# Value products in 64x32 tiles, exponentials in three tiles of 512, and the pair ring in free-first order

## The chip, the core and the metric

The kernel runs on one core of one Trainium2 chip. The metric is device time in microseconds, the median of several executions. Shorter is better.

## The reference

One layer mixes a sliding-window attention A and a dense MLP B, both on the same x (2048 rows of 512), by a gate that is one number per row:

```python
x = A_x
g = sigmoid((x * gate_w).sum(-1, keepdims=True))
# A: 32 heads of 16, causal, each query sees itself and the 255 keys before it
qkv = (x @ wqkv).reshape(B, S, 3, H, Dh)            # S = 2048, D = 512
scores = einsum("bhqd,bhkd->bhqk", q, k) * (Dh ** -0.5)
mask = (i - j >= 0) & (i - j < 256)
p = softmax(where(mask, scores, -1e9))
a = (einsum("bhqk,bhkd->bhqd", p, v)).reshape(B, S, D) @ wo
# B: F = 1792
b = gelu(x @ w1 + b1) @ w2 + b2
return g * a + (1 - g) * b
```

## The kernel before, in words

**Two kinds of work on TensorE.** The dense products (query/key and value projections `qk` and `v`, MLP `u` and `y`, output projection `a`) split each fp32 operand into a rounded high part and a remainder, and add three products. They run as pairs of matmuls with 64 contraction rows each, 512 columns wide: rows 0 to 63 work on one output bank and rows 64 to 127 on another, side by side (`half`, L689 to L702; `Dense`, which chooses what each half does next). The attention runs in 32 units, one for each of 4 query blocks of 512 (c) and 8 groups of 4 heads (g_).

**One attention unit.** (1) `att_max` (`sm`, L865) computes scores of 128 queries by 384 keys, and VectorE finds each query's maximum (L871, L872). (2) `att_rows` writes the negated maxima as extra rows of the queries, so that the next product comes out with them subtracted. (3) `att_exp` (`st`, L928) computes the scores again with keys on partitions and queries on the free axis, ScalarE takes the exponential into a tile `pt` (L933), and GpSimd zeroes the triangles of it that the window excludes (L937, two calls a tile). A unit sees up to six key blocks kb = 0 to 5 of 128 keys; block 2 is the first one of the query block itself. `PARTS` lays them out in four tiles of 384 queries a head pair: kb 0 and 1 (128 and 256 queries), kb 2 (384), kb 3 (384), kb 4 and 5 (256 and 128). (4) `att_pv` (`pv`, L957) multiplies values by exponentials: four heads in four 128x32 column tiles of the array, 128 key rows each, all six key blocks accumulated in one bank of ring `d`. These operands are plain fp32, and the trace has two matmul records for each such matmul, called passes below. (5) ScalarE copies the bank out (L970), a DMA sends it to `ND`, and numerators and denominators go through DRAM to the division. In the 8 units of c = 0, kb 0 and 1 do not exist: tile 0 is left out there.

**PSUM.** Ring `d` has 4 banks, used by the dense groups and by `pv`. Ring `sc` has 2 pairs of banks, used by `sm` and `st`, and by the transposes of x.

**Order of the work.** All five queues are filled by a planner in the kernel itself (`Plan`, with `op`, `pe`, `ready`, `advance`): every operation carries a cost in ns, and the planner writes each engine's program in the order that its own clock makes ready. The main loop gives TensorE, at each step, either the next attention item (`score_items` lists them in one fixed order) when its inputs and its bank are ready by the plan and attention is due, or a pair of dense halves, or one half alone. At run time each queue is in order, so an instruction whose semaphore is late holds what stands behind it on its engine. `Ring` gives buffers out in turn; `Slots` gives the buffer that comes free first.

**The end.** After the last `pv`, dense halves of the output projection `a` of the third query block fill TensorE while the last heads go through `att_last` (DRAM, reciprocal, product, split). Then come 48 matmuls of 128 rows (`whole`, L803) for the last query block, of which the last 12 need the last heads.

Of the kernel before, what the change touches and what calls it, by code (L numbers as in the profile page):

```python
# [18 lines left out]
T = 512  # L19
NT = S // T  # L20
NB = T // 128
# [5 lines left out]
SCALE = DH ** -0.5  # L27
# [144 lines left out]
def gated_mix(ctx: ExitStack, tc: tile.TileContext, x, wqkv, wo, w1, b1, w2, b2, gate_w, out):  # L172
    nc = tc.nc
    x = x[0]
    out = out[0]
# [8 lines left out]
    plan = Plan()  # L184
    op, pe = plan.op, plan.pe
# [133 lines left out]
    def load_two(k, prio):  # L319
        tag = "pt" if k < 2 * NB else "raw"  # L320

        def start(n):
            for i in (n, n + 1) if n == k else ():
                if tag == "pt":
                    v = new("pt", [128, 2, 384], F32, f"xr{i}", toks["xr", i], toks["z", i])
# [387 lines left out]
    class Dense:  # L713
# [1 line left out]


        def __init__(self, groups):
            self.groups, self.at, self.opened = groups, 0, 0
# [14 lines left out]
        def ready(self, g_, r):  # L733

            group = self.groups[g_]
            t = plan.ready(needs(group.mms[self.k[r][g_]][0]), [rings["d"]] if group.p is None else [])
            if t is None:
                return None
            return max(t, self.touch[1 - r][g_] + APART)
# [171 lines left out]
    PARTS = [[(0, 0, 128), (1, 0, 256)], [(2, 0, 384)], [(3, 128, 384)], [(4, 256, 256), (5, 384, 128)]]  # L911

    def parts_at(j):
        return [(*p, sum(v[2] for v in PARTS[j][:n])) for n, p in enumerate(PARTS[j])]

    def att_exp(i, j, pr):
        q, k = qbuf[:, i % QB], kbuf[:, i % QB]
        rel, box = Tok(), []

        def go():  # L920
            pt = new("pt", [128, 2, 384], F32, f"pt{i}_{j}_{pr}", toks["pv", i])
            pts[i, j, pr] = pt
            p = pair(f"st{i}_{j}_{pr}", rel)
            box.extend((pt, p))
            for kb, lo, w, at in sorted(parts_at(j), key=lambda v: -v[2]):
                for s in range(2):
                    rows_ = slice(64 * s, 64 * s + KR)
                    nc.tensor.matmul(p[:, s, at:at + w], k[rows_, pr, kb * 128:(kb + 1) * 128],  # L928
                                     q[rows_, pr, lo:lo + w], start=True, stop=True, skip_group_check=True)
        done = pe(SPAIR + (0 if j in (1, 2) else 46), go)  # L930
        if j == 3 and pr == 1:
            toks["stacks", i].t = done.t
        op({"ACT": 810.0}, lambda e: nc.scalar.activation(box[0], box[1][:, :, :384], AF.Exp, scale=SCALE), [done], 0, rel)  # L933

        def keep(at, upper):
            v = box[0][:, :, at:at + 128]
            nc.gpsimd.affine_select(out=v, in_=v, pattern=[[0, 2], [1 if upper else -1, 128]], compare_op=ALU.is_ge,  # L937
                                    fill=0.0, base=0 if upper else -1, channel_multiplier=-1 if upper else 1)
        k0 = op({"POOL": 440.0}, lambda e: keep(0, j > 0), [rel], 2)
        op({"POOL": 440.0}, lambda e: keep(256, j == 3), [k0], 2, toks["pt", i, j, pr])  # L940

    def att_pv(i):
        c, g_ = combos[i]
        vt = vbuf[:, i % 2]
        rel, box = Tok(), []
        tiles = range(1 if c == 0 else 0, 4)
        cost = 2950 if c else 2300

        def go():
            pv = bank(f"pv{i}", rel, tag=PVT)  # L950
            box.append(pv)
            first = True
            for j in tiles:
                at = 0
                for n, (kb, lo, w) in enumerate(PARTS[j]):
                    for h in range(4):
                        nc.tensor.matmul(pv[32 * h:32 * h + 32, lo:lo + w],  # L957
                                         vt[:, 68 * kb + 17 * h:68 * kb + 17 * h + 32],
                                         pts[i, j, h // 2][:, h % 2, at:at + w],
                                         start=first, stop=j == 3 and n == 1,  # L960
                                         skip_group_check=True, tile_position=(0, 32 * h))
                    first = False
                    at += w
        done = pe(cost, go)
        toks["pv", i].t = done.t
        box2 = []

        def ev(e):
            box2.append(new("tmp", [128, T], F32, f"nd{i}", sent))
            nc.scalar.activation(box2[0], box[0], AF.Copy)  # L970
        sent = ND_T[i] = Tok()
        te = op({"ACT": 595.0}, ev, [done], EVP[4], rel, [rings["tmp"]])
# [70 lines left out]
    def score_items():  # L1043

        NU = len(combos) * NB
        for u in range(-LEAD, NU):
            i, j = divmod(u, NB)
            mi, mj = divmod(u + LEAD, NB)
            if mj == LOADAT and mi + AHEADQ < len(combos):
                yield 0, [], [], lambda mi=mi: att_load(mi + AHEADQ), 0  # L1050
            if j == 0 and i >= 0:
                yield 0, [], [], lambda i=i: att_load_v(i), 0
            for pr in range(2):
                if mi < len(combos):
# [3 lines left out]
                if i >= 0 and (j > 0 or combos[i][0] > 0):  # L1058
                    yield 180, [toks["rows", i]], [rings["sc"], rings["pt"]], lambda i=i, j=j, pr=pr: att_exp(i, j, pr), 1
                if i > 0 and j == PVAT and pr == 0:  # L1060
                    yield 2700, pv_needs(i - 1), [rings[PVT]], lambda i=i: att_pv(i - 1), 2
        yield 2700, pv_needs(NU // NB - 1), [rings[PVT]], lambda: att_pv(NU // NB - 1), 2

    def pv_needs(i):
        js = range(1 if combos[i][0] == 0 else 0, 4)
        return [toks["lv", i]] + [toks["pt", i, j, pr] for j in js for pr in range(2)]


    def main():
# [17 lines left out]
        box = []  # L1087
# [16 lines left out]
            att_load(i)  # L1104
        dense = Dense(groups)
        score = score_items()
        A_all = 128 * 2 * (176 + 184) + 32 * 2700.0
        a_at = 0.0
        a = next(score, None)
        LEADA = dense.total * (1 - ENDS)  # L1110
# [2 lines left out]
        while a or not dense.over():  # L1113
# [14 lines left out]
            ra = plan.ready(a[1], a[2]) if a else None  # L1128
            can = dense.pick(t)
            a_ok = ra is not None and ra <= t  # L1130
            due = a and (dense.over() or a_at / A_all <= dense.spent / LEADA)
# [89 lines left out]
```

## Time and profile before

| what | value |
|---|---|
| median of 3 runs | 714.04 us (713.48 to 714.2) |
| the profiled execution | 715.14 us |
| its span, first to last instruction | 713.4 us |
| TensorE busy | 99% of the span |
| VectorE, ScalarE, GpSimd busy | 73%, 66%, 60% |
| granted TensorE clock | 1.00 |

How to read the rows of the prediction: PE is TensorE's matmuls, PEld its weight loads, DVE VectorE, ACT ScalarE, POOL GpSimd. A group's row has the line, engine, operation, output<-inputs, shapes, the count, then busy time in us, mean ns of one, and idle time ahead of them with what ended it. A timeline row begins with the start and the length in us; a chain row likewise. A row of waits has: who waited <- for whom: us in total, times, longest.

### The profile page before, as it was taken

To read this page: it belongs to the slowest core of one execution; us is meant where nothing else is said; L and a number is where in the kernel's file an instruction comes from. 1 tells how busy PE (TensorE), PEld (TensorE's weight loads), DVE (VectorE), ACT (ScalarE), POOL (GpSimd) and SP (SyncE) were. 2 spreads that over 40 slices of the span, in tenths; PEclk is the share of its full clock that TensorE was granted. 3 is DMA by queue.
4 is the path that set the end of the run, shared out by engine and by line. 5 is a ranking of instruction groups with operands and counts; after the bars stand their busy time and mean duration, and the time that the engine had idled before them with its cause. 6 is when DMAs were issued, how large, how long until landed. Compare 5 with 4: busy or idle time off the path is not lost.

```text
span 713.4 us, 18412 instructions
## 1 busy us (share of the span) xinstructions
PE 703.7 (99%) x6819; PEld 589.4 (83%) x6819; DVE 521.5 (73%) x994; ACT 473.1 (66%) x776; POOL 425.4 (60%) x777
## 2 busy tenths in 40 slices
PE   9999999999999999999999999999999999999997
PEld 7899888778887788978877888878888888878776
DVE  6377778968777886796754677895876877778655
ACT  5746688748867865865654678875875886775800
POOL 5234559755856974774633567892774896684700
PEclk9999999999999999999999999999999999999999
DMA  8896888187666666666959988765778677755554
GB/s 294 209 272 202 218 270 249 49 220 223 135 131 119 133 143 152 146 173 150 247 199 224 250 241 213 183 200 134 194 183 163 149 178 171 177 197 188 182 193 151
DMA packets 104616, 133.89 MB, mean 188 GB/s; under 512 B 38472, under 2 KB 53840, under 8 KB 104528
## 3 DMA queue, kind: packets, MB, share of 16 engines
q1 hardware_dynamic: 104528, 132.73, 70.4%
q8 instruction: 54, 0.88, 0.6%
q14 instruction: 34, 0.28, 0.1%
HBM read 82.39 MB, written 50.30 MB: 186 GB/s over the span
## 4 chain that ended last, share of the span: by engine, by line
PE 88%; DVE 3%; POOL 3%; DMA 2%; ACT 1%; issue 1%; SPq 1%; POOLq 0%; DVEq 0%; ACTq 0%
PE y L699 21%; PE u L699 19%; PE pv L957 11%; PE qk L699 10%; PE sm L865 7%; PE st L928 5%; PE v L699 5%; PE a L699 5%; PE a L803 2%; POOL qbuf L907 1%; DMA kbuf<-SK 1%; PE v L803 1%; PE qk L803 1%; PE xp L359 1%; DMA rb<-RD 1%
## 5 line engine op out<-in xcount | busy, mean ns | idle before, releaser
L937 POOL TENSOR_SCALAR_AFFINE_SELECT pt<-pt 128x256 f32<-128x256 f32 x480 | 215.0, 473 | 170.6 <-ACT pt L933 166.5
L933 ACT ACTIVATE pt<-st 128x768 f32<-128x768 f32 x240 | 194.0, 810 | 92.6 <-PE st L928 87.0
L699 PE MATMUL y<-w,h 64*128 64x512 f32 x1344 | 220.2, 397 | 0.0
L699 PEld LDWEIGHTS y<-w,h 64*128 64x128 f32 x1344 | 157.2, 185 | 13.4 <-PE y L699 1.5
L871 DVE COPY_PREDICATED sm<-lower,sm 128x256 f32<-128x256 uint8 x224 | 95.0, 424 | 92.0 <-PE sm L865 84.8
L699 PE MATMUL u<-xt,w 64*128 64x512 f32 x1008 | 161.3, 395 | 0.1
L872 DVE TENSOR_REDUCE M<-sm 128x2 f32<-128x512 f32 x224 | 154.9, 691 | 7.7
L699 PEld LDWEIGHTS u<-xt,w 64*128 64x128 f32 x1008 | 118.7, 185 | 6.8 <-PE u L699 0.7
L699 PE MATMUL qk<-xt,qk 64*128 64x512 f32 x720 | 109.9, 395 | 0.0
L865 PE MATMUL sm<-kbuf,qbuf 56*128 56x384 f32 (+2 forms) x512 | 106.3, 353 | 2.3 <-DVE xt L363 0.8
L928 PE MATMUL st<-qbuf,kbuf 56*128 56x256 f32 (+2 forms) x704 | 96.3, 284 | 0.2
L907 POOL CAST qbuf<-tt 8x256 fp32r<-8x256 f32 x171 | 78.9, 462 | 22.8 <-PE st L928 5.9
L501 POOL TENSOR_TENSOR h<-x1h,h 128x512 fp32r<-128x512 f32 x56 | 77.1, 1379 | 20.5 <-ACT h L491 20.0
L699 PEld LDWEIGHTS qk<-xt,qk 64*128 64x128 f32 x720 | 84.3, 185 | 5.4 <-ACT xr L369 0.4
L957 PE MATMUL pv<-pt,vbuf 128*32 128x384 f32 (+2 forms) x1408 | 84.3, 386 | 1.0 <-ACT x1h L474 1.0
L865 PEld LDWEIGHTS sm<-kbuf,qbuf 56*128 56x128 f32 x512 | 62.4, 184 | 23.8 <-issue 10.9
L928 PEld LDWEIGHTS st<-qbuf,kbuf 56*128 56x128 f32 x704 | 77.9, 186 | 4.3 <-POOL qbuf L907 0.8
L957 PEld LDWEIGHTS pv<-pt,vbuf 128*32 128x32 f32 x1408 | 41.5, 110 | 44.9 <-issue 29.5
L699 PE MATMUL u<-mx,w 64*128 64x512 f32 x336 | 59.3, 397 | 0.0
L487 DVE SCALAR_TENSOR_TENSOR x1h<-sqh,x1h 128x512 f32<-128x512 f32 x56 | 49.0, 880 | 7.7 <-ACT sqh L497 7.3
L484 DVE SCALAR_TENSOR_TENSOR sqh<-sqh,x1h 128x512 f32<-128x512 f32 x56 | 49.2, 882 | 2.8 <-ACT sqh L479 2.8
L474 ACT ACTIVATE x1h<-u,b1c 128x512 f32<-128x512 f32 x56 | 38.4, 686 | 17.4 <-PE u L699 12.4
(85 smaller groups left out, 816.9 us busy)
## 6 DMA issues: line engine op xcount, KB each, us to landing
kbuf<-SK SPq DMA_DIRECT2D x48, 192.0 KB
SQ<-qke SPq DMA_DIRECT2D x16, 512.0 KB
SK<-qke SPq DMA_DIRECT2D x16, 512.0 KB
qbuf<-SQ SPq DMA_DIRECT2D x64, 128.0 KB
ND<-nd SPq DMA_DIRECT2D x32, 256.0 KB
raww<-in_B_w_dram SPq DMA_DIRECT2D x28, 256.0 KB
kbuf<-SK SPq DMA_DIRECT2D x48, 96.0 KB
SV<-vx SPq DMA_DIRECT2D x16, 272.0 KB
```

The costliest lines, as they stand in the source:

```text
L484: nc.vector.scalar_tensor_tensor(box["q"], box["q"], GC, box["x"], op0=ALU.add, op1=ALU.mult)
L487: nc.vector.scalar_tensor_tensor(box["x"], box["q"], 1.0, box["x"], op0=ALU.add, op1=ALU.mult)
L501: lambda e: ENG[e].tensor_sub(hts[name][:, 1], box["x"], f32(hts[name][:, 0])), [t5], gp, toks["h", name])
L699: ins = nc.tensor.matmul(wide(group.p, rhs), lhsT[rows_], rhs[rows_], start=group.left == n, stop=group.left == 1, skip_group_check=True)
L865: nc.tensor.matmul(p[:, s, :w], q[rows_, pr, j * 128:(j + 1) * 128], k[rows_, pr, at:at + w], start=True, stop=True)
L871: nc.vector.copy_predicated(p[:, :, 0:128], lower.unsqueeze(1).broadcast_to([128, 2, 128]), p[:, :, 256:384])
L872: nc.vector.tensor_reduce(M[:, j, 2 * pr:2 * pr + 2], p[:, :, 0:256], AXES, ALU.max)
L907: nc.gpsimd.tensor_copy(dst, src)
L928: nc.tensor.matmul(p[:, s, at:at + w], k[rows_, pr, kb * 128:(kb + 1) * 128], q[rows_, pr, lo:lo + w], start=True, stop=True, skip_group_c ...
L933: op({"ACT": 810.0}, lambda e: nc.scalar.activation(box[0], box[1][:, :, :384], AF.Exp, scale=SCALE), [done], 0, rel)
L937: nc.gpsimd.affine_select(out=v, in_=v, pattern=[[0, 2], [1 if upper else -1, 128]], compare_op=ALU.is_ge, fill=0.0, base=0 if upper else ...
L957: nc.tensor.matmul(pv[32 * h:32 * h + 32, lo:lo + w], vt[:, 68 * kb + 17 * h:68 * kb + 17 * h + 32], pts[i, j, h // 2][:, h % 2, at:at + w ...
```

## The change

1. `att_exp` makes three tiles of up to 512 queries a head pair in place of four of 384: kb 1 with kb 4 (256 and 256), kb 2 with kb 0 (384 and 128), kb 3 with kb 5 (384 and 128). For c = 0 the first is kb 4 alone (256) and the second kb 2 alone (384). GpSimd's zeroing takes two calls a tile, three 128-blocks in two of the tiles.
2. `att_pv` cuts each key block in two halves of 64 keys. Each half runs in its own 64x32 tiles, so eight in all, with its own bank, and covers the 320 queries that its 64 keys can reach instead of 384. The lower half (s = 0) takes the key blocks upward, the upper half (s = 1) downward. The output is a pair of ring `sc` instead of a bank of `d`; ScalarE copies the first bank out and VectorE adds the second to it.
3. Ring `sc` becomes `Slots`. There are 8 exponential tiles of 4 KB a partition instead of 11 of 3 KB, the planner's LAT is 145 instead of 120 ns, LEAD (by how many blocks the maxima run ahead) 6 instead of 5, and the costs that the planner has for these operations are new. HOLD at -1e9 leaves the new `dense.hold` at 0 throughout.

```diff
     def pair(name, *rel):
         rings["sc"].take(*rel)
+        if "sc" in SLOTS:
+            return ps.tile([128, 2, T], F32, tag=f"sc{rings['sc'].i}", bufs=1, name=name)
...
+    def parts_at(c, j):
+        if j == 0:
+            ps_ = [(1, 0, 256, 0), (4, 256, 256, 256)]
+            tri = [(128, 1, False), (256, 1, True)]
+        elif j == 1:
+            ps_ = [(2, 0, 384, 0), (0, 0, 128, 384)]
+            tri = [(0, 1, True), (256, 2, False)]
+        else:
+            ps_ = [(3, 128, 384, 128), (5, 384, 128, 0)]
+            tri = [(0, 2, True), (384, 1, False)]
+        if c == 0 and j < 2:
+            ps_ = [v for v in ps_ if v[0] > 1]
+            tri = [(0, 1, True), (256, 1, False)] if j else tri[1:]
+        return ps_, tri
...
-        op({"ACT": 810.0}, lambda e: nc.scalar.activation(box[0], box[1][:, :, :384], AF.Exp, scale=SCALE), [done], 0, rel)
+        op({"ACT": 170.0 + 0.835 * 2 * (c1 - c0)}, lambda e: nc.scalar.activation(box[0][:, :, c0:c1], box[1][:, :, c0:c1], AF.Exp, scale=SCALE),
+           [done], 0, rel)
...
-            pv = bank(f"pv{i}", rel, tag=PVT)
+                pv = pair(f"pv{i}", rel)
+                pv = [pv[:, 0], pv[:, 1]]
...
+            for n in range(len(pieces)):
+                for h in range(4):
+                    for s in range(2):
+                        j, kb, lo, w, at = pieces[last - n if s else n]
+                        off = lo - 128 * (kb - 2)
+                        skip = 0 if c == 0 and kb == 2 else max(0, 64 * s - off)
+                        wide_ = min(off + w, 320 + 64 * s) - off - skip
+                        rows_ = slice(64 * s, 64 * s + 64)
+                        nc.tensor.matmul(pv[s][32 * h:32 * h + 32, lo + skip:lo + skip + wide_],
+                                         vt[rows_, 68 * kb + 17 * h:68 * kb + 17 * h + 32],
+                                         pts[i, j, h // 2][rows_, h % 2, at + skip:at + skip + wide_],
+                                         start=n == 0, stop=n == last,
+                                         skip_group_check=True, tile_position=(64 * s, 32 * h))
...
-            nc.scalar.activation(box2[0], box[0], AF.Copy)
+            nc.scalar.activation(box2[0], box[0][0], AF.Copy)
+
+        def both(e):
+            nc.vector.tensor_add(box2[0], box2[0], box[0][1])
...
+            t0 = op({"ACT": 595.0}, ev, [done], EVP[4], rels[0], [rings["tmp"]])
+            te = op({"DVE": 690.0}, both, [t0], EVP[4], rels[1])
+            join([te], rel)
...
-BUFS = {"d": 4, "e": 1, "sc": 2, "h": 9, "raw": 3, "x1": 3, "sq": 2, "ya": 2, "w": 14, "pt": 11, "xt": 2, "tmp": 3, "tt": 1, "M": 2, "den": 2}
-LAT = 120.0
+BUFS = {"d": 4, "e": 1, "sc": 2, "h": 9, "raw": 3, "x1": 3, "sq": 2, "ya": 2, "w": 14, "pt": 8, "xt": 2, "tmp": 3, "tt": 1, "M": 2, "den": 2}
+LAT = 145.0
...
-LEAD = 5
+LEAD = 6
...
-PVT = "d"
-SLOTS = ("d", "h", "x1", "raw", "tmp", "ya", "sq")
+PVT = "sc"
+PVN = 1
+PV2 = True
+STS = ((0, 0), (0, 1), (1, 1), (2, 0), (2, 1), (3, 1))
+HOLD = -1e9
+PVC = 2523.0
+PVC0 = 2090.0
+SLOTS = ("d", "sc", "h", "x1", "raw", "tmp", "ya", "sq")
```

With three tiles a head pair instead of four, a unit with c > 0 has six `st` items instead of eight. The widths of its pieces in `att_pv`, in the order in which a half takes them, are 64, 192, 320, 320, 256, 128 for both halves; before, they were 128, 256, 384, 384, 256, 128. For c = 0 they are 320, 320, 256, 128 for the lower half and 64, 192, 320, 384 for the upper; before, 384, 384, 256, 128.

On TensorE, before, the value product of unit 12 (`pv12`; `pt12_j_p` is the exponential of tile j and head pair p) stands as one run of 24 matmuls, each row here being two heads:

```order
L957 MATMUL pv12_4894<-pt12_0_0_4478,vbuf_139 32x128 x2
L957 MATMUL pv12_4894<-pt12_0_1_4511,vbuf_139 32x128 x2
L957 MATMUL pv12_4894<-pt12_0_0_4478,vbuf_139 32x256 x2
L957 MATMUL pv12_4894<-pt12_0_1_4511,vbuf_139 32x256 x2
L957 MATMUL pv12_4894<-pt12_1_0_4543,vbuf_139 32x384 x2
L957 MATMUL pv12_4894<-pt12_1_1_4591,vbuf_139 32x384 x2
```

Now, on the same engine, a piece of unit 13's product: the last matmuls of 64 queries, the pieces of 192, and the first of 320:

```order
L1000 MATMUL pv13_5418<-pt13_1_1_5220,vbuf_139 32x64
L1000 MATMUL pv13_5418<-pt13_2_1_5323,vbuf_139 32x64
L1000 MATMUL pv13_5418<-pt13_0_0_5009,vbuf_139 32x192 x4
L1000 MATMUL pv13_5418<-pt13_0_1_5051,vbuf_139 32x192 x4
L1000 MATMUL pv13_5418<-pt13_1_0_5188,vbuf_139 32x320
L1000 MATMUL pv13_5418<-pt13_2_0_5263,vbuf_139 32x320
```

The matmuls of the lower and upper half alternate, and there are 48 of them for a unit with c > 0 instead of 24, 32 instead of 16 for c = 0. All other matmuls of the program are the same in number and shape.

On VectorE, now, at the same unit: `sm15_3_1` is the score product that stands right behind `pv13` on TensorE, `nd13` the sum of the two banks, `sm16_0_0` the next product that is given `pv13`'s pair:

```order
L873 COPY_PREDICATED sm15_3_0_5413<-lower_144,sm15_3_0_5413 128x2x128
L874 TENSOR_REDUCE M15_5215<-sm15_3_0_5413 128x2
L873 COPY_PREDICATED sm15_3_1_5473<-lower_144,sm15_3_1_5473 128x2x128
L874 TENSOR_REDUCE M15_5215<-sm15_3_1_5473 128x2
L1014 TENSOR_TENSOR nd13_5480<-nd13_5480,pv13_5418 128x512
L892 TENSOR_SCALAR nm_138<-M15_5215 128x4x4
L893 SCALAR_TENSOR_TENSOR nm_138<-M15_5215,nm_138 128x4x4
L895 STREAM_TRANSPOSE tt15_5509<-nm_138 128x128
L873 COPY_PREDICATED sm16_0_0_5516<-lower_144,sm16_0_0_5516 128x2x128
```

The addition `nd13` is new on VectorE; it stands behind the reduction of the product that follows `pv13`. On TensorE there are 20 dense halves and one `st` item between `sm15_3_1` and `sm16_0_0`.

More of the change, by code (lines that the diff above doesn't have):

```diff
@@ L735, in ready @@
             group = self.groups[g_]
-            t = plan.ready(needs(group.mms[self.k[r][g_]][0]), [rings["d"]] if group.p is None else [])
+            t = plan.ready(needs(group.mms[self.k[r][g_]][0]), [rings["d"]] * (1 + self.hold) if group.p is None else [])
             if t is None:
@@ L924, in go @@
             box.extend((pt, p))
-            for kb, lo, w, at in sorted(parts_at(j), key=lambda v: -v[2]):
+            for kb, lo, w, at in ps_:
                 for s in range(2):
@@ L929, in go, with keep @@
                                      q[rows_, pr, lo:lo + w], start=True, stop=True, skip_group_check=True)
-        done = pe(SPAIR + (0 if j in (1, 2) else 46), go)
-        if j == 3 and pr == 1:
+        done = pe({512: 250.0 if j == 0 else 283.0, 384: 184.0, 256: 130.0}[c1 - c0], go)
+        if j == 2 and pr == 1:
             toks["stacks", i].t = done.t
[L933 to L937, printed above, removed]
+        op({"ACT": 170.0 + 0.835 * 2 * (c1 - c0)}, lambda e: nc.scalar.activation(box[0][:, :, c0:c1], box[1][:, :, c0:c1], AF.Exp, scale=SCALE),
+           [done], 0, rel)
+        def keep(at, n, upper):
+            v = box[0][:, :, at:at + 128 * n]
+            if n == 2:
+                v = v.rearrange("p s (n q) -> p s n q", n=2)
+            nc.gpsimd.affine_select(out=v, in_=v, pattern=[[0, 2], [1 if upper else -1, 128]] if n == 1 else
+                                    [[0, 2], [0, 2], [1 if upper else -1, 128]], compare_op=ALU.is_ge,
                                     fill=0.0, base=0 if upper else -1, channel_multiplier=-1 if upper else 1)
-        k0 = op({"POOL": 440.0}, lambda e: keep(0, j > 0), [rel], 2)
-        op({"POOL": 440.0}, lambda e: keep(256, j == 3), [k0], 2, toks["pt", i, j, pr])
+        last = rel
+        for n, v in enumerate(tri):
+            last = op({"POOL": 160.0 + 280 * v[1]}, lambda e, v=v: keep(*v), [last], 2,
+                      toks["pt", i, j, pr] if n == len(tri) - 1 else None)
     def att_pv(i):
@@ L945, in att_pv @@
         rel, box = Tok(), []
-        tiles = range(1 if c == 0 else 0, 4)
-        cost = 2950 if c else 2300
-        def go():
-            pv = bank(f"pv{i}", rel, tag=PVT)
-            box.append(pv)
[L952 to L963, printed above, removed]
@@ L964, in att_pv, with go1 @@
-        done = pe(cost, go)
+        cost = PVC if c else PVC0
+        rels = Tok(), Tok()
+        pieces = sorted(((j, *v) for j in range(3) for v in parts_at(c, j)[0]), key=lambda v: v[1])
+        def go1():
+            pv = bank(f"pv{i}", rel)
+            box.append([pv])
+            for n, (j, kb, lo, w, at) in enumerate(pieces):
+                for h in range(4):
+                    nc.tensor.matmul(pv[32 * h:32 * h + 32, lo:lo + w],
+                                     vt[:, 68 * kb + 17 * h:68 * kb + 17 * h + 32],
+                                     pts[i, j, h // 2][:, h % 2, at:at + w], start=n == 0, stop=n == len(pieces) - 1,
+                                     skip_group_check=True, tile_position=(0, 32 * h))
@@ new lines, in go @@
+        def go():
+            if PVT == "sc":
+                pv = pair(f"pv{i}", rel)
+                pv = [pv[:, 0], pv[:, 1]]
+            else:
+                pv = [bank(f"pv{i}_{s}", rels[s]) for s in range(2)]
+            box.append(pv)
+            last = len(pieces) - 1
+            for n in range(len(pieces)):
+                for h in range(4):
+                    for s in range(2):
[9 more added lines that the diff above has]
+                                         skip_group_check=True, tile_position=(64 * s, 32 * h))
@@ L965, in att_pv @@
+        done = pe(cost, go if PV2 else go1)
         toks["pv", i].t = done.t
@@ L1057, in score_items @@
                         lambda mi=mi, mj=mj, pr=pr: att_max(mi, mj, pr), 1
-                if i >= 0 and (j > 0 or combos[i][0] > 0):
-                    yield 180, [toks["rows", i]], [rings["sc"], rings["pt"]], lambda i=i, j=j, pr=pr: att_exp(i, j, pr), 1
+                if i >= 0 and (j, pr) in STS:
+                    n, r = divmod(STS.index((j, pr)), 2)
+                    yield 180, [toks["rows", i]], [rings["sc"], rings["pt"]], lambda i=i, n=n, r=r: att_exp(i, n, r), 1
                 if i > 0 and j == PVAT and pr == 0:
-                    yield 2700, pv_needs(i - 1), [rings[PVT]], lambda i=i: att_pv(i - 1), 2
-        yield 2700, pv_needs(NU // NB - 1), [rings[PVT]], lambda: att_pv(NU // NB - 1), 2
+                    yield 2300, pv_needs(i - 1), [rings[PVT]] * PVN, lambda i=i: att_pv(i - 1), 2
+        yield 2300, pv_needs(NU // NB - 1), [rings[PVT]] * PVN, lambda: att_pv(NU // NB - 1), 2
     def pv_needs(i):
-        js = range(1 if combos[i][0] == 0 else 0, 4)
-        return [toks["lv", i]] + [toks["pt", i, j, pr] for j in js for pr in range(2)]
+        return [toks["lv", i]] + [toks["pt", i, j, pr] for j in range(3) for pr in range(2)]
     def main():
@@ L1106, in main @@
         score = score_items()
[L1107 removed]
+        A_all = 128 * 2 * (176 + 184) + 32 * 2300.0
         a_at = 0.0
@@ L1128, in main @@
             ra = plan.ready(a[1], a[2]) if a else None
+            dense.hold = 0
+            if a and a[4] == 2:
+                rv = plan.ready(a[1])
+                dense.hold = PVN if rv is not None and rv <= t + HOLD else 0
             can = dense.pick(t)
```

16 lines of the change are left out of this document (9 added, 7 removed).

## Prediction

> **What bounds the kernel now.** I read the page first: the busy shares, the granted clock, and the chain that ended last by engine.
>
> ```profile
> span 713.4 us, 18412 instructions
> PE 703.7 (99%) x6819; PEld 589.4 (83%) x6819; DVE 521.5 (73%) x994; ACT 473.1 (66%) x776; POOL 425.4 (60%) x777
> PEclk9999999999999999999999999999999999999999
> PE 88%; DVE 3%; POOL 3%; DMA 2%; ACT 1%; issue 1%; SPq 1%; POOLq 0%; DVEq 0%; ACTq 0%
> ```
>
> TensorE is busy for 703.7 of 713.4 us at full clock, and 88% of the chain is its own work. So the time is the sum of what TensorE streams, and only 9.7 us are gaps. Work taken off ScalarE, GpSimd or VectorE gains nothing unless TensorE waits for it.
>
> Next, the chain in order of time, for the value products: two of the c = 0 kind, then the first and the last of the 24 units with c > 0.
>
> ```profile
> 87.10 2.08 PE pv L957 x32
> 101.84 2.08 PE pv L957 x32
> ...
> 227.48 2.73 PE pv L957 x48
> 676.57 2.73 PE pv L957 x48
> ```
>
> A unit costs 2.08 us (8 units, c = 0) or 2.73 us (24 units), together 8 x 2.08 + 24 x 2.73 = 82.2 us. The length is that of the pieces' widths. The timeline of one unit shows it: the first row is the product, the others are its weight loads, four at a time, one for each column tile.
>
> ```profile
> 339.46 2.80 PE L957 MATMUL pv<-pt,vbuf 128*32 128x128 f32 x48
> 339.60 0.13 PEld L957 LDWEIGHTS pv<-pt,vbuf 128*32 128x32 f32 x4
> 339.71 0.13 PEld L957 LDWEIGHTS pv<-pt,vbuf 128*32 128x32 f32 x4
> 340.46 0.13 PEld L957 LDWEIGHTS pv<-pt,vbuf 128*32 128x32 f32 x4 [0.19 <-issue]
> 340.79 0.13 PEld L957 LDWEIGHTS pv<-pt,vbuf 128*32 128x32 f32 x4 [0.19 <-issue]
> 341.11 0.13 PEld L957 LDWEIGHTS pv<-pt,vbuf 128*32 128x32 f32 x4 [0.19 <-issue]
> 341.43 0.56 PEld L957 LDWEIGHTS pv<-pt,vbuf 128*32 128x32 f32 x12 [0.19 <-issue]
> ```
>
> Each group of loads starts with a pass. Passes of 384 queries follow each other after 0.323 us (340.46 to 341.43 in three steps), so a column costs 0.00084 us, with four tiles at once and nothing lost between them. A pass of 128 takes 0.11 us (339.60 to 339.71), which is 128 columns at that rate.
>
> **The value products.** Let a pass cost 0.00084 us a column, and each width two passes. Now, for c > 0, the widths 128, 256, 384, 384, 256, 128 give 2 x 2 x (0.11 + 0.215 + 0.323) = 2.59 us; the row has 2.73, so 0.14 is entry and exit. For c = 0: 2 x (0.323 + 0.323 + 0.215 + 0.11) = 1.94, and 2.08 again leaves 0.14.
>
> After the change each half streams its own widths. A 64-wide pass would stream 0.054 us, but weights must be loaded between two passes of a tile:
>
> ```profile
> L957 PEld LDWEIGHTS pv<-pt,vbuf x1408: 106/110/110, 71.0 to 678.9; 128*32 128x32 f32 x176
> ```
>
> A load of 32 columns takes 110 ns, and the trace shows no pass shorter than that, so I take 0.11 for the 64-wide pass, with 0.054 as the other end. For c > 0: 2 x (0.11 + 0.161 + 0.269 + 0.269 + 0.215 + 0.11) = 2.27, plus 0.14, is 2.41 us: 0.32 less than 2.73. For c = 0 both halves come to 2 x 0.863 = 1.73, plus 0.14, is 1.87: 0.21 less than 2.08. Sum: 24 x 0.32 + 8 x 0.21 = 9.4 us less. With 0.054 it is 24 x 0.43 + 8 x 0.21 = 12.0.
>
> The Trainium skill ("TensorE: Matmul & The Clock Gate", section on LDWEIGHTS) gives a load's time as its columns divided by 1.2 in ns, an estimated 27 ns for 32 columns; by that the 64-wide pass would not be held and the sum would be the 12.0. The row has 110 ns, so the trace does not agree as far as a single load's duration goes, and I stay with it.
>
> No row shows 32-column tiles with 64 rows. The upper bound of the cost comes from the rows at the end of the program, where 64-row pairs and whole 128-row matmuls of the same 512 columns stand side by side:
>
> ```profile
> 679.22 19.38 PE L699 MATMUL a<-wo,ot 64*128 64x512 f32 x154
> 698.53 11.20 PE L803 MATMUL a<-wo,ot 128*128 128x512 f32 x48
> ```
>
> A pair takes 2 x 19.38 / 154 = 0.252, a whole one 0.233 us: at most 0.019 us for the split, some of which may be waits. On 12 passes (c > 0) and 8 (c = 0) that takes back 24 x 0.23 + 8 x 0.15 = 6.7 us and leaves 2.7. I take no such tax, since the pass rows lose nothing to the column split and the term is only a bound: 9.4, ends 2.7 and 12.0.
>
> For c = 0 the sum supposes that a half goes on when the other is behind, since the widths beside each other differ (320 with 64, 320 with 192, 256 with 320, 128 with 384). The trace has such a place:
>
> ```profile
> 330.85 0.36 PE L928 MATMUL st<-qbuf,kbuf 56*128 56x256 f32 x3
> 331.03 0.44 PE L699 MATMUL y<-w,h 64*128 64x512 f32 x1
> 331.06 0.22 PE L928 MATMUL st<-qbuf,kbuf 56*128 56x128 f32 x1
> ```
>
> `att_exp` issues its four matmuls together, before any dense one; yet a `y` half starts at 331.03, ahead of the last `st` at 331.06. One half was free and did not wait for the other. The Trainium skill (the same page, "The mechanism" in its part on packing small matmuls) says that matmuls start and end strictly in program order. By that rule the sum would be the first rival's; the trace speaks against it here.
>
> **The rest on TensorE.** All other matmuls are the same. A count of both orders gives 60 instead of 40 dense halves with no partner. Each costs between nothing (the halves run apart, as just seen) and half a pair, 0.126 us: 0 to 2.5 us, taken 1.2.
>
> **Entry into the product.** The mode of the array changes at each `pv` in both programs, equally often; its cost lies in the 0.14 and in what precedes 339.46, and I move neither.
>
> **Other engines.** These rows price them:
>
> ```profile
> L933 ACT ACTIVATE pt<-st 128x768 f32<-128x768 f32 x240 | 194.0, 810 | 92.6 <-PE st L928 87.0 <-POOL pt L937 3.5
> L970 ACT ACTIVATE nd<-pv 128x512 f32<-128x512 f32 x32 | 19.0, 593 | 30.4 <-PE pv L957 26.9 <-issue 3.3
> L363 DVE TENSOR_TENSOR xt<-xp,xt 128x512 fp32r<-128x512 f32 x16 | 10.5, 683 | 11.6 <-ACT xt L362 11.6
> L872 DVE TENSOR_REDUCE M<-sm 128x2 f32<-128x512 f32 x224 | 154.9, 691 | 7.7
> L871 DVE COPY_PREDICATED sm<-lower,sm 128x256 f32<-128x256 uint8 x224 | 95.0, 424 | 92.0 <-PE sm L865 84.8 <-PE st L928 5.1 <-ACT x1h L474 0.4
> L484 DVE SCALAR_TENSOR_TENSOR sqh<-sqh,x1h 128x512 f32<-128x512 f32 x56 | 49.2, 882 | 2.8 <-ACT sqh L479 2.8
> L937 POOL TENSOR_SCALAR_AFFINE_SELECT pt<-pt 128x256 f32<-128x256 f32 x480 | 215.0, 473 | 170.6 <-ACT pt L933 166.5
> ```
>
> Exponentials: 810 ns for 768 elements and 593 for 512 (a copy) give 0.85 ns an element, so about 1.03 us for 1024. ScalarE's total falls from 194 to about 187 us, by 7. GpSimd has 368 calls in place of 480, 64 of them of double width. VectorE gains 32 additions like the 683 ns of L363, 22 us or 3% of the span. All are covered by TensorE's stream at 60 to 76% load: cost 0. Without that cover, the exponential that `pv` waits for would come 0.22 us later a unit, 7 us in all.
>
> **PSUM and waits.** The product no longer takes a dense bank, which can only help TensorE's 9.7 us of gaps; 3.7 of those lie after the last matmul (span 713.4; the chain has its last step from 709.76, below), so at most 6 are there to win. Taken 0, end 3. In exchange it holds one of two pairs until VectorE has added the second bank. The item that gets this pair next waits for it on TensorE, and everything dense behind it waits too. At `pv13` the addition stands on VectorE behind a predicated copy and a reduction: sm (0.45, from 342.19 in the row below), 0.42, 0.69, then 0.68, so 2.2 us after the product's end. TensorE meanwhile has `sm`, 20 dense halves at 0.126 and one `st`, at least 2.5 us. Covered by 0.3 us or more; cost 0.
>
> ```profile
> 342.19 0.45 PE L865 MATMUL sm<-kbuf,qbuf 56*128 56x384 f32 x2
> 701.20 0.90 DVE L583 TENSOR_TENSOR ot<-nr,ot 64x128 fp32r<-64x128 f32 x4
> 709.76 0.75 DVE yb L618
> ```
>
> **The end.** The way from the last `pv` to the division grows by the addition, 0.7 us. Its last step is done at 702.1; the 37th of the 48 last matmuls needs it at 698.53 + 36 x 0.233 = 706.9. By the orders, 199 dense halves follow the last product instead of 154: 5.7 us more cover. Cost 0. LEAD, LAT and the number of exponential tiles move places in the orders only: cost 0, within the ends above.
>
> **Sum.** Span 713.4 - 9.4 + 1.2 = 705.2. The profiled execution took 715.14 us, 1.7 more than its span, and the median is 714.04, 1.1 less than that execution; so the median becomes 714.0 - 8.2 = 705.8 us.
>
> **The rivals.** *Halves in step (chance 0.10).* If the two halves start in program order, a c = 0 unit costs the larger width of each couple: 2 x (0.269 x 3 + 0.323) + 0.14 = 2.40 in place of 2.08. Eight units lose 2.6 us, the gain is 24 x 0.32 - 2.6 = 5.1, and the time 714.0 - 5.1 + 1.2 = 710.1. For it: the two halves are issued alternately. Against it: 331.03 above.
>
> *A tax on every pass (0.09).* Gain 2.7, time 714.0 - 2.7 + 1.2 = 712.5. For it: no row has eight tiles. Against it: four column tiles lose nothing.
>
> *The held pair becomes the bound (0.10), slower.* Place: the item that takes over the product's pair. If one 0.88 us VectorE operation like L484 stands ahead of the addition in every unit, it is free 3.1 us after the product, against 2.5 of work: 0.6 x 31 = 19 us lost, so 705.8 + 19 = 725. It decides from 8.2 / 31 = 0.26 us a unit on. For it: 0.3 us is a narrow cover, and VectorE is 73% busy. Against it: ScalarE sat idle for 26.9 us waiting for `pv` (L970), so the copy starts at once, and the planner gives both steps its first priority.
>
> *No eightfold overlap (0.02).* If the halves ran one after the other, a unit with c > 0 would cost 2 x 2.27 + 0.14 = 4.7 us, 2.0 more, and the time would be about 760. Against it: the dense halves overlap.
>
> *More than forecast (0.06).* Weight loads hide in the 64-wide passes (12.0) and 3 us of gaps go: 714.0 - 12.0 - 3 = 699.
>
> **How the numbers follow.** The forecast has 0.63, with 702.0 (12.0 gained, 0 for lone halves) to 712.5 as its own ends. The range 701 to 713 takes it in with the first two rivals, and leaves out 0.18. A measurement of this kernel can tell about 0.2%, 1.4 us, from no change. Faster by more: the forecast, the first rival, half of the tax and the last one, 0.63 + 0.10 + 0.05 + 0.06 = 0.84. Slower: 0.12, less what a mild wait of the pair would leave near zero, 0.11. Within: 0.05.
>
> **What would show it.** Right: in the chain, `pv` at 2.4 us (c > 0) and 1.87 (c = 0); a 64-wide pass of 0.11; TensorE's busy share still 99%; the dense rows unchanged. Wrong: `pv` over 2.6 us; `pv` for c = 0 at 2.4 while the others are at 2.4 (halves in step); waits of `sm` or `st` for `nd` of over 8 us in total; or TensorE below 98%.

## The result, and the profile after

The changed kernel takes 706.95 us (median of four runs, 705.5 to 708.76), the kernel before 714.12 on the same chip (713.48 to 715.27). The ratio is 0.9889, 95% interval 0.9868 to 0.991: faster by 1.1%. The profiled execution took 705.5 us, with a span of 703.8. It is the fastest of the four, and the profiled execution of the kernel before (715.14) lies 1 us above its median, so the two profiles are 9.6 us apart where the medians are 7.2 apart. All sums from traces below are of such single executions.

The page of the changed kernel, the same lines as before:

```profile
span 703.8 us, 21178 instructions
PE 692.0 (98%) x8227; PEld 588.0 (84%) x8227; DVE 543.8 (77%) x1034; ACT 463.4 (66%) x722; POOL 396.4 (56%) x663
PEclk9999999999999999999999999999999999999999
PE 85%; DMA 6%; DVE 4%; issue 2%; SPq 1%; POOL 1%; ACT 1%; DVEq 0%; POOLq 0%
```

TensorE is still the bound at full clock, with 1,408 passes more (the page counts two for each of these matmuls) and 11.7 us less busy. The chain now runs through loads for 6% of the span, yet TensorE stands idle for only 11.8 us. Next the chain in order of time: a c = 0 unit, a c > 0 unit, then the last one with what follows it.

```profile
72.94 2.15 PE pv L1000 x45
...
247.55 2.32 PE pv L1000 x96
...
661.21 2.33 PE pv L1000 x96
663.53 25.42 PE a L701 x195
688.95 11.14 PE a L805 x48
700.09 0.03 issue
700.12 0.75 DVE yb L620
```

A unit with c > 0 went from 2.73 to 2.32 us (forecast 2.41). A unit with c = 0 went from 2.08 to 2.15: it became slower, where 1.87 was forecast. Two of the 24 longer units took much more, as the timeline of TensorE shows for the one at 341 us (start, duration, and in brackets the idle time ahead of the row):

```profile
341.26 2.36 PE L1000 MATMUL pv<-pt,vbuf 64*32 64x64 f32 x87
344.94 0.43 PE L1000 MATMUL pv<-pt,vbuf 64*32 64x128 f32 x9 [1.33 <-issue]
345.30 0.45 PE L867 MATMUL sm<-kbuf,qbuf 56*128 56x384 f32 x2
```

This unit lasted 345.30 - 341.26 = 4.04 us; the other, at 401.15, lasted 3.28. Nothing that the profile records released the last nine matmuls ("issue").

To see where the time went I add up, over the trace's matmuls, the time from the start of each to the start of the next, by what it computes. All sums below are made this way, in us; "stalled" is what single units took beyond the usual length of their kind (in the last two rows waits and a lower clock are part of it; the 1.7 of "old product, lead 6" are a lower clock, 0.62 granted from 657.3 to 661.8 us, a lower clock is in part of the 26.3 of "pieces cut in two", and 1.9 of the 3.0 of "two dense banks" are waits for ScalarE and VectorE). The rows from the third on are the experiments below.

```
                                         value products  of it stalled  all other matmuls
before                                        82.1            0              626.1
after                                         75.7           2.7             622.8
c = 0 halves in one direction                 70.8            0              622.9
both halves always in one direction           71.5            0              622.0
old widths, split in eight tiles              86.9           2.0             620.3
pieces cut in two                            115.3          26.3             629.0
planner's costs mended                        72.2           1.3             624.1
old product, lead 6                           83.8           1.7             633.1
old product, lead 5                           82.1            0              630.5
new product, lead 5                           73.1           0.1             630.7
pair in turn                                  73.0            0              621.7
two dense banks                               76.0           3.0             638.3
product alone, in turn                        80.9           7.9             652.3
product alone, free first                     78.6           5.5             640.2
```

The product gave 24 x 0.403 = 9.7 us at c > 0, lost 8 x 0.075 = 0.6 at c = 0 and 2.7 in two stalls: 6.4 net. The other 3.3 of the 9.6 between the two profiles come from all other matmuls, which are the same in number and shape and stand in another order. That the order made them is not shown: the third to fifth row have the changed kernel's order, and their rest still goes from 620.3 to 622.9, and 2.4 of the 9.6 are not in the medians.

ScalarE and GpSimd answer as forecast: the exponentials have 186.0 us in 192 calls (194.0 in 240), the selections 193.9 in 368 (215.0 in 480).

```profile
L956 POOL TENSOR_SCALAR_AFFINE_SELECT pt<-pt 128x256 f32<-128x256 f32 (+1 forms) x368 | 193.9, 550 | 138.1 <-ACT pt L949 128.0
L949 ACT ACTIVATE pt<-st 128x1024 f32<-128x1024 f32 (+2 forms) x192 | 186.0, 970 | 86.7 <-PE st L944 81.4
```

For the pair that the product holds, the view of the tile `pv` (who waited for it, us and times) has no wait of TensorE; ScalarE and VectorE only wait within the chain product, copy, addition:

```profile
L1014 DVE TENSOR_TENSOR nd<-nd,pv x32: 620/677/689, 75.8 to 664.3; 128x512 f32<-128x512 f32 x32
...
who waited for it (us, times):
  ACT nd L1011: 37.3, 22
  DVE nd L1014: 0.7, 1
```

### The profile page after: what moved, and what is told of

The parts are those of the page before. It is cut to its first block, busy times and chain, and to the rows that moved or that the text cites. A ratio compares the mean times of both kernels' runs of the same rounds, so it can differ in the third digit from the quotient of the medians.

```text
span 703.8 us, 21178 instructions
## 1 busy us (share of the span) xinstructions
PE 692.0 (98%) x8227; PEld 588.0 (84%) x8227; DVE 543.8 (77%) x1034; ACT 463.4 (66%) x722; POOL 396.4 (56%) x663
## 4 chain that ended last, share of the span: by engine, by line
PE 85%; DMA 6%; DVE 4%; issue 2%; SPq 1%; POOL 1%; ACT 1%; DVEq 0%; POOLq 0%
PE y L701 20%; PE u L701 20%; PE pv L1000 9%; PE qk L701 9%; PE sm L867 6%; PE st L944 6%; PE a L701 5%; PE v L701 4%; DMA qbuf<-SQ 3%; PE a L805 2%; PE v L805 1%; DMA SV<-vx 1%; PE qk L805 1%; PE xp L361 1%; DVE w L315 1%
## 5 line engine op out<-in xcount | busy, mean ns | idle before, releaser
L956 POOL TENSOR_SCALAR_AFFINE_SELECT pt<-pt 128x256 f32<-128x256 f32 (+1 forms) x368 | 193.9, 550 | 138.1 <-ACT pt L949 128.0
L949 ACT ACTIVATE pt<-st 128x1024 f32<-128x1024 f32 (+2 forms) x192 | 186.0, 970 | 86.7 <-PE st L944 81.4
L701 PE MATMUL y<-w,h 64*128 64x512 f32 x1344 | 228.4, 397 | 0.7 <-DVE w L315 0.7
L701 PE MATMUL u<-xt,w 64*128 64x512 f32 x1008 | 168.6, 394 | 0.0
L867 PE MATMUL sm<-kbuf,qbuf 56*128 56x384 f32 (+2 forms) x512 | 98.7, 346 | 1.8 <-DVE M L874 1.2
L944 PE MATMUL st<-qbuf,kbuf 56*128 56x384 f32 (+1 forms) x704 | 82.4, 284 | 2.1 <-DVE M L874 1.7
L1000 PE MATMUL pv<-pt,vbuf 64*32 64x320 f32 (+5 forms) x2816 | 76.3, 348 | 1.8 <-issue 1.7
L867 PEld LDWEIGHTS sm<-kbuf,qbuf 56*128 56x128 f32 x512 | 56.5, 184 | 21.8 <-issue 11.1
L1000 PEld LDWEIGHTS pv<-pt,vbuf 64*32 64x32 f32 x2816 | 48.4, 106 | 29.2 <-issue 8.7
L701 PE MATMUL v<-v,xt 64*128 64x512 f32 x288 | 53.0, 394 | 0.0
```

The source lines that it names most:

```text
L701: ins = nc.tensor.matmul(wide(group.p, rhs), lhsT[rows_], rhs[rows_], start=group.left == n, stop=group.left == 1, skip_group_check=True)
L867: nc.tensor.matmul(p[:, s, :w], q[rows_, pr, j * 128:(j + 1) * 128], k[rows_, pr, at:at + w], start=True, stop=True)
L949: op({"ACT": 170.0 + 0.835 * 2 * (c1 - c0)}, lambda e: nc.scalar.activation(box[0][:, :, c0:c1], box[1][:, :, c0:c1], AF.Exp, scale=SCALE) ...
L1000: nc.tensor.matmul(pv[s][32 * h:32 * h + 32, lo + skip:lo + skip + wide_], vt[rows_, 68 * kb + 17 * h:68 * kb + 17 * h + 32], pts[i, j, h ...
```

## The experiments

My theory after the result: two sizes of the forecast were wrong in opposite directions, the 64-wide pass (not held by its load) and the c = 0 units (the halves are not free of each other over a whole unit). The rivals: the order of the work, and not the product, made the gain; a tax on the split; the stalls as chance. The kernel before had medians of 714.3, 713.73 and 715.22 us beside the three groups of runs.

### The halves: which of them waits for which

```diff
-                        j, kb, lo, w, at = pieces[last - n if s else n]
+                        j, kb, lo, w, at = pieces[last - n if s and c else n]
```

> For c = 0 alone both halves take the key blocks upward, so that widths beside each other are near equal (320 with 384, 320 with 320, 256 with 192, 128 with 64); all other instructions stand as they did. If the 2.15 us of these units come from one half being held by the other in the order of issue, they fall to 1.87 to 2.03 us, 1.0 to 2.3 us in all: 704.7 to 706.0 beside 707.0 of the changed kernel. If it is a fixed cost of the 64x32 form (entry, exit, more instructions), they stay at 2.15 and the time stays at 707. Units with c > 0 stay at 2.33 either way.

Measured: 704.64 us (700.73 to 707.42, six runs), ratio 0.9861 (0.9834 to 0.9889). The chain of the profiled run:

```profile
72.87 1.88 PE pv L1000 x54
89.48 1.88 PE pv L1000 x54
```

So 1.88 us, the forecast length, once the two pieces beside each other differ by at most 64 columns. Eight units give 2.2 us, and the median is 2.3 below the changed kernel's, though the two intervals overlap. With both halves in one direction for c > 0 as well (`pieces[n]`):

> Both halves take the key blocks upward in all units, so for c > 0 the widths beside each other differ: 64 with 128, 192 with 256, 320, 320, 256 with 192, 128 with 64. Each half has the same sum as before. If halves are independent, pv at c > 0 stays at 2.33 us. If they go in step, the sum of the larger widths is 1408 instead of 1280 columns, 2 x 128 x 0.00084 = 0.215 us more: 2.54, and 5 us more in all. Units with c = 0 as in the run before.

The one run took 700.52 us. A c > 0 unit takes 2.350 us from its first matmul to the next one behind it, against 2.325, and 2.54 if the halves went in step. A difference of 64 columns thus costs 0.025 us a unit. In the changed kernel the halves of a c = 0 unit differ by up to 256 columns and lose 2.153 - 1.882 = 0.27 us. The records of the changed kernel's unit at 72.87 show how: the upper half's second pass of 192 starts at 73.179 and would be through at 73.34 at 0.00084 us a column, but its pass of 320 starts at 73.63, when the lower half is a pass further. The 0.29 us between are the loss. A half can run ahead of the other, but only by so much; what sets the distance is not shown.

### The old widths in eight tiles

```diff
-                        skip = 0 if c == 0 and kb == 2 else max(0, 64 * s - off)
-                        wide_ = min(off + w, 320 + 64 * s) - off - skip
+                        skip = 0
+                        wide_ = w
```

Each half computes all 384 queries of a key block, which are zeros in part; the order is the changed kernel's on all engines.

> Eight 64x32 tiles as in the change, but each half streams all queries of its key block (128, 256, 384, 384, 256, 128), zeros included; the order on every engine is as in the changed kernel. If the gain comes from 320 in place of 384 queries, pv at c > 0 is 2.70 to 2.80 us, the time 714 to 718. If the split into eight tiles itself makes the product faster, pv stays below 2.6.

Measured: 712.94 us (ten runs, 711.74 to 716.66), ratio 0.9988 (0.9973 to 1.0003), no difference from before, and 1 us below the 714 to 718 expected. The chain:

```profile
73.57 2.37 PE pv L1000 x47
...
249.20 2.75 PE pv L1000 x96
```

The same columns in eight 64x32 tiles take 2.752 us where four 128x32 tiles took 2.728: the split costs 0.024 us a unit, 0.6 us in all, against the 6.7 of the rival with a tax. The c = 0 units, whose halves differ by 256 columns here too, take 2.37 in place of 2.08. The narrower pieces are worth 712.94 - 706.95 = 6.0 us by the medians; the two profiles, 8.7 us apart, have 86.9 - 75.7 = 11.2 in the product and 2.5 of it lost again in a rest that has the same order.

### The number of instructions in a unit

The first experiment's kernel, with each piece of 192 columns or more at c > 0 cut in two matmuls: the same columns, 80 matmuls a unit instead of 48.

```diff
+                        for m in (0, 1) if c and wide_ >= 192 else (0,):
+                            x0 = skip + m * wide_ // 2
+                            x1 = skip + wide_ // 2 if c and wide_ >= 192 and m == 0 else skip + wide_
...
```

> Run e1 with each piece of 192 queries or more cut in two at c > 0: the same columns and the same sums, 80 matmuls a unit in place of 48, so 12 more packets of 16 KB of instructions. If late refills of TensorE's instructions make the stalls inside pv and the scatter of the times, more units have a stall without a releaser inside pv, their sum is above 4 us, and the median is 4 to 12 us above run e1. If they don't, pv grows by 0.05 us or less a unit and the median stays within 2 us of run e1.

Measured: 745.24 us (742.47 to 751.22), ratio 1.0427 (1.0396 to 1.0459): 40.6 us above the first experiment, where 4 to 12 were expected. The profiled execution is the slowest of the four. Its chain shows a unit of the shortest kind, the timeline one of the 13 longer ones:

```profile
229.12 3.08 PE pv L1003 x141
```

```profile
247.68 2.93 PE L1003 MATMUL pv<-pt,vbuf 64*32 64x64 f32 x146
253.09 0.46 PE L1003 MATMUL pv<-pt,vbuf 64*32 64x128 f32 x14 [2.48 <-issue]
253.48 0.69 PE L867 MATMUL sm<-kbuf,qbuf 56*128 56x384 f32 x2
```

The same columns take 3.08 us in place of 2.32 even in a unit without a stall. Each of the 80 matmuls is two passes with a load ahead of each, 320 records a unit, so 9.6 ns for one on the mean; what sets this rate is not shown, since at the start of the changed kernel's unit at 247.48 twenty loads and passes start within 49 ns. On top of that 13 units stalled, the longest of them 7.4 us from end to end. And after each of the five idle gaps of over 2 us (2.05 to 2.74) the granted clock was 0.50 for 3.4 us, as from 253.4, which the rest of the kernel pays too (629.0 in place of 622.9). So more matmuls for the same columns cost in three ways: the mean rate, the stalls and the clock behind the longest of them. For the stalls, the changed kernel's own DMA rows make the loading of instructions a suspect. The DMA view of the window 340 to 346 us, in which the stalled unit lies, has one packet of the instruction queue:

```profile
q8 instruction: 1, 0.02, 1.7%
```

1.7% of 16 engines over 6 us is 1.6 us for this one packet of 16 KB; its record runs from 341.84, inside the unit, and the packet from 400.21 (1.89 us) reaches into the other stalled unit, which starts at 401.15. A c > 0 unit now spends 192 records in 2.3 us, 96 in 2.7 before. That more records a unit bring stalls is shown; that a late packet is what TensorE waits for is not. All 13 stalled units of this run and both of the changed kernel have such a packet in them, but so have 9 of the 11 and 9 of the 22 other units with c > 0: most of the 66 packets of the changed kernel (54 before) stop nothing. Nor do stalls come in every execution alike, it seems: the first experiment's profile is the fastest of its six runs (700.73, the slowest 707.42) and has none.

### The product and what came with it

Four kernels take the change apart. First the old product (one bank, 384 queries) in the changed kernel's surroundings: three tiles of 512, the free pair first, LEAD 6, LAT 145.

```diff
...
-PVT = "sc"
+PVT = "d"
...
-PV2 = True
+PV2 = False
...
-PVC = 2523.0
-PVC0 = 2090.0
+PVC = 2950.0
+PVC0 = 2300.0
```

> The new exponential tiles, ring and planner's constants, with the value product as it was: 128x32 tiles, 384 queries, one bank of ring d. If the gain is the product's stream, pv is back at 2.73 and 2.08 us and the time at 713 to 715. If the exponentials in three tiles, the free-first pairs or the new constants bring part of the gain, the time stays below 711.

Measured: 722.61 us, ratio 1.0102 (1.0075 to 1.0129): slower than before, which neither expectation had. The value products are as before but for one at a lower clock, and the rest has 633.1 us in place of 626.1. Its waits name loads:

```profile
PE sm L867 <- DMA qbuf<-ZR: 6.6, 4, 1.9
```

The same with `LEAD = 5`, as in the kernel before:

> The run with the old product in the new surroundings (one bank, 384 queries, three tiles of 512; 722.6 us) with one number changed: the maxima run five units ahead of the exponentials, as in the kernel before, and not six. Theory A, the sixth unit ahead is what costs: its score products then wait for loads of qbuf (gaps of 1.8, 2.1, 2.1 and 1.4 us ahead of sm at 303.6, 471.1, 508.1 and 546.0 us), and score products held TensorE 61.7 us against 51.0 before; without it the 8 us go and the time is 713 to 716 us. Theory B, three tiles of 512 and the pair taken free first cost this with the old product whatever the lead: it stays at 720 to 724 us.

Measured: 719.63 us, ratio 1.007 (1.0044 to 1.0096). The waits for loads are gone; the longest in the list of TensorE's waits is now:

```profile
PE sm L867 <- DVE M L874: 2.5, 4, 1.0
```

So theory A explains the waits but not the time: the sixth unit ahead costs the old product 2 to 3 us at most (the two intervals overlap), and the other surroundings leave it 0.7% slower than before, which is nearer to theory B. Now the changed kernel with `LEAD = 5`:

> The changed kernel with one number changed: maxima five units ahead, not six. If the sixth unit ahead does nothing for the new product, the time stays within a few us of 707 (705 to 710). If the sixth unit is what keeps the product in pairs of banks fed (its exponentials wait for rows that come from maxima), the attention falls behind dense work and the time is over 715. If the sixth unit costs here as it may with the old product, 700 to 703 us.

Measured: 710.67 us, ratio 0.9939 (0.9918 to 0.9961), just above the first of the three. Against the run above this changes the product alone, and it is worth 719.63 - 710.67 = 9.0 us; the sums say the same, 82.1 - 73.1 = 9.0 for the product, and 630.5 against 630.7 for the rest. The sixth unit ahead is then worth 710.67 - 706.95 = 3.7 us to the new product (0.9939 against 0.9889, intervals apart).

And the new product in the kernel before (four tiles of 384, LEAD 5, LAT 120, pairs in turn):

```diff
-            pv = bank(f"pv{i}", rel, tag=PVT)
...
+            pv = pair(f"pv{i}", rel)
...
```

> The kernel before with the new value product alone (64x32 tiles, two banks in a pair of ring sc, addition on VectorE); four exponential tiles, pairs in turn, LAT 120 and LEAD 5 as before. If the stream of the product is all of the gain, pv is 2.33 and about 2.15 us and the time 704 to 708. If the tiles of 512 or the free-first pairs are needed for it, the score items wait for the held pair and the time is above 710.

Measured: 742.38 us, ratio 1.0403 (1.0373 to 1.0433): 28 us slower. The windows at its end (length, then busy us of TensorE and its loads, VectorE, ScalarE, GpSimd; then the granted clock, the share of the DMA engines and GB/s) show where, and behind them stand three rows of TensorE's timeline there:

```profile
680.00:700.00 20.00, 9.72 (x136) 6.01 (x134) 15.99 (x23) 9.37 (x15) 7.31 (x18) 0.74 0.41 133
700.00:720.00 20.00, 15.39 (x226) 11.00 (x227) 5.25 (x6) 8.37 (x12) 8.22 (x20) 0.67 0.08 28
720.00:740.00 20.00, 10.81 (x40) 7.88 (x38) 11.63 (x19) 1.64 (x5) 0.00 (x0) 0.85 0.22 79
```

```profile
711.36 0.39 PE L964 MATMUL pv<-pt,vbuf 64*32 64x64 f32 x2 [0.17 <-issue]
713.28 0.44 PE L964 MATMUL pv<-pt,vbuf 64*32 64x64 f32 x8 [1.53 <-POOL pt L937]
714.09 3.64 PE L964 MATMUL pv<-pt,vbuf 64*32 64x64 f32 x86 [0.37 <-POOL pt L937]
```

From 680 us on TensorE is busy for 35.9 of 58.4 us. The dense halves are used up by 682.4 us, while the last three value products (684.57, 702.74 and 711.36) are still to come: the last one starts at 711.36 and waits for its own exponentials' selections, where in the changed kernel it starts at 661.21 and has 195 dense halves behind it. What stands in the open is the chain of exponentials, product, copy, addition, transfer and division. The granted clock is at 0.67 to 0.85 there too. TensorE has no wait for the addition in this run either; its largest waits there are for maxima, query rows, exponentials and selections.

### The free pair first

In the changed kernel the pairs are taken strictly in turn:

```diff
-SLOTS = ("d", "sc", "h", "x1", "raw", "tmp", "ya", "sq")
+SLOTS = ("d", "h", "x1", "raw", "tmp", "ya", "sq")
```

> The changed kernel with the two pairs of banks taken strictly in turn and not free first, nothing else. Theory A, the product alone in the old surroundings took 742.4 us for want of the free pair first (a pair that waits for the product's eviction and add holds the next taker though the other pair is free): then this one loses most of that too and takes 725 to 745 us. Theory B, it was the four tiles of 384 instead of three of 512, with 8 takings of a pair a unit and 0.8 us of work in each instead of 6: then this one stays within 5 us of 707.

Measured: 702.0 us (701.72 to 704.53), ratio 0.9828 (0.98 to 0.9856), the lowest median of the versions with more than one run: some 4 to 5 us faster than the change as made (by the two ratios 4.4, by the medians 5.0). This version together with the first experiment's edit was not tried. In the profiled executions, 3.8 us apart, no unit stalls here (2.7 of the difference), and the rest has 621.7 us in place of 622.8, a difference that kernels with one order show too. The reverse edit, free first for the product alone:

> The run with the new product alone in the old surroundings (four tiles of 384; 742.4 us) with the pair of banks that is free taken first. Theory A, in turn or free first decides: 710 to 720 us. Theory B, the number of takings of a pair decides (8 pairs of exponentials a unit in place of 6): 735 to 745 us.

Measured: 724.33 us, ratio 1.0135 (1.0108 to 1.0162), 18 us less than in turn, and still slower than before. The end is less open:

```profile
680.00:700.00 20.00, 16.69 (x251) 12.97 (x255) 10.83 (x15) 9.74 (x16) 9.06 (x22) 0.86 0.43 140
700.00:720.00 20.00, 14.78 (x73) 10.91 (x56) 12.46 (x19) 2.24 (x6) 0.00 (x0) 0.76 0.14 51
```

Neither theory holds in both places. The same rule gains 18 us where attention comes late and loses 4 to 5 where it doesn't. Three tiles of 512 (with their 8 buffers) and LAT 145 are together worth 724.33 - 710.67 = 13.7 us to the new product; I have not separated them.

### Two smaller ones

Two dense banks for the product, with dense work held back until both are free (`PVT = "d"`, `PVN = 2`, `HOLD = 0.0`):

> The changed kernel with the product's two banks taken from ring d instead of a pair of ring sc; the planner holds dense work back for them (HOLD at 0) and makes its own order. If the pair of ring sc was a cheap place, as the prediction had it, the product stays at 2.33 us a unit and TensorE waits more for dense banks: 708 to 716. If the held pair costs the changed kernel several us, this version is faster than 705.

Measured: 720.81 us, ratio 1.0099 (1.0084 to 1.0114). The product's lengths are unchanged (2.325 and 2.153), the rest has 638.3 us, and the time is above the 708 to 716 expected: with this planner the pair is the cheaper place.

The first experiment's kernel with the planner's costs of a unit nearer to the measured lengths (`PVC = 2430.0`, `PVC0 = 1990.0`):

> Run e1 with the planner's costs of the product set to what the trace shows (2.325 + 0.105 and 1.88 + 0.11 us, entry included), which gives another order. Both theories expect pv as in e1; if the planner's cost matters by its size, 0.1 us x 32 = 3 us at most: 701 to 705; else as e1, 704.6.

Measured: 703.99 us (702.19 to 704.09), ratio 0.9856 (0.984 to 0.9872), the same as with the old costs within their scatter.

## Why the prediction came out, point by point

The number is close, 705.8 forecast for 706.95, because errors of both signs met: that is luck. Between the profiles the forecast's 9.4 gained and 1.2 lost stand against 9.7 gained at c > 0, 0.6 lost at c = 0, 2.7 lost in stalls and 3.3 gained in the rest; by the medians 2.4 less came of it.

**The 64-wide pass: mis-sized.** I held it at 0.11 us by its load's row. In the unit at 247.48 the first passes of 64 start at 247.479, the second ones at 247.559 and the first passes of 192 at 247.615. So the first takes 80 ns and the second 56, close to the 0.054 that it streams, while the load's row still has its old duration:

```profile
L1000 PEld LDWEIGHTS pv<-pt,vbuf x2816: 102/107/108, 72.9 to 663.2; 64*32 64x32 f32 x188
```

So the recorded duration of a load is not the time for which it holds the tile. Here the rule of the Trainium skill that the prediction weighed ("TensorE: Matmul & The Clock Gate", section on LDWEIGHTS) was the better price: by the 27 ns estimated from it the pass is not held, and the trace now agrees with that, at 56 ns for the second pass; no row shows the 27 ns themselves. The gain at c > 0 is 9.7 us and not 7.7.

**The c = 0 units: wrong in sign.** I let a half go on whenever the other is behind, on the strength of one place in the trace. That shows that a half can start ahead, not by how much. With 64 columns of difference it holds (1.882 measured, 1.87 forecast; 2.350 for c > 0), with 256 it doesn't: 0.6 us lost, 1.7 forecast as gain. The strict program order that the Trainium skill states (same page, "The mechanism") would have given 2.40 and 2.54; 2.153 and 2.350 lie between that and independence.

**The tax: right at nothing.** 0.024 us a unit.

**Instructions: not in the sum.** No step counted a cost of twice as many matmuls a unit. In the profiled run stalls took 2.7 us; in the other kernels with 48 matmuls a unit and no open end they took between 0 and 2.0, waits left out.

**Lone halves: not visible.** The 1.2 us I charged cannot be seen in a rest that fell by 3.3.

**The held pair: right for this kernel, by a wrong reason.** TensorE never waits for `nd`, but my cover of 0.3 us a unit isn't what decides. With the old tiles, LEAD and pairs in turn TensorE doesn't wait for it either, yet attention ends up behind the dense work and the kernel is 28 us slower, at the end and not in each unit. That is the slower rival by its outcome, not by its place.

**"LEAD, LAT and the number of exponential tiles: cost 0": the step that failed.** With this product, LEAD 6 is worth 3.7 us, tiles and LAT 13.7, and the free pair first, which no step priced, costs 4 to 5. Those are terms as large as the whole forecast. With the old product the surroundings cost 5 to 7 (0.7% and 1.0%). Taken as nothing they came out at 3.3 us of gain in the two profiles, and the medians leave less; that they came out near nothing is chance. Why the rest takes 622 us in one order and 630 in another I have not settled; it shows in no single wait.

**The end: right.** The last matmul starts 4.1 us before the end of the span in both kernels, and 195 dense halves cover the addition.

## What to carry to other kernels

Price a short pass by its columns, not by the recorded duration of its weight load, and give tiles that share the array pieces of like width at the same time. Splitting a product in more tiles costs next to nothing in streaming, but its instructions do count: 48 matmuls in 2.3 us went, 80 did not. A sum made from two profiles explains those two executions: see how far each lies from its median before crediting a few us to a cause. When an edit comes with new numbers for the planner, try it in the old surroundings and the old one in the new before crediting either: here the product was worth 9.0 us in one setting and minus 28 in the other.

## What the hardware showed beside that

A unit of 320 records (loads and passes) took 3.08 us, 9.6 ns for each on the mean, where the same columns in 192 records took 2.32. One instruction packet of 16 KB took from 0.9 to 2.5 us in the trace of the changed kernel. Two row halves can drift apart by a 64-column piece for 0.025 us a unit, but pieces that differ by up to 256 columns cost 0.27. And the granted clock was 0.67 on the mean in a stretch where TensorE was busy for 15.4 of 20 us, behind one in which it was busy for 9.7, which makes an open end longer than its waits. With the pieces cut in two, idle gaps of 2.05 to 2.74 us were enough for 3.4 us at 0.50.
